# State-space convolution gated with linear attention, one core: inputs turned by TensorE instead of by DMA, the query side in blocks of 512 rows beside the first kernel channels, ScalarE table groups given explicitly

## The chip, the cores and the metric

One NeuronCore of one Trainium2 chip runs the whole program. The metric is the device time of one execution in microseconds (us). A profiled execution comes with it: its span goes from the first to the last instruction, and its whole time is a little longer. The engines are PE (TensorE; PEld is its weight loading), DVE (VectorE), ACT (ScalarE), POOL (GpSimd) and SP (SyncE); each has its own queue and works it off in order. "ACTq" and "SPq" are the queues' DMA issues.

## The reference

Two sequence operators on the same x (2048 rows, 512 columns, bf16), mixed by a gate per row:

```python
x = A_u
g = sigmoid((x * gate_w).sum(-1, keepdims=True))
# A: long convolution, its kernel K from a diagonal state space (128 states a channel)
dt = exp(log_dt)[:, None]; logdA = dt * (A_re + 1j * A_im); dB = dt * (B_re + 1j * B_im)
K = einsum("dn,dnl,dn->dl", C_re + 1j * C_im, exp(logdA[:, :, None] * arange(L)), dB).real
a = irfft(rfft(pad(x.T)) * rfft(pad(K)))[:L].T + x * Dskip
# B: linear attention, 32 heads of 16, features softmax(+p) and softmax(-p)
q, k, v = split(x @ wqkv); pq = q @ w_phi; pk = k @ w_phi
phi = lambda p: concat([softmax(p), softmax(-p)])
kv = einsum("sf,sd->fd", phi(pk), v); z = phi(pk).sum(0)
b = ((phi(pq) @ kv) / (phi(pq) @ z + 1e-6)) @ wo
return g * a + (1 - g) * b
```

## The kernel before

**Convolution.** It is a Fourier transform made of matmuls: stage a (`fft_stage_a`) multiplies with W1, stage b (`fft_stage_b`) with the tables TB, and each result is cast from PSUM to SBUF by an `Evict`, which gives its casts to DVE ("v", L68) and ACT ("a", L70) by a pattern. The input's spectrum XU is made once (`u_path`: 16 tiles of stage a into XAu, 16 of stage b into XU), from UD, which holds x with 64 rows per partition. The convolution kernel K is made for 128 channels at a time (`Q`, four blocks). For a block: E, the exponentials (L277, eight ACT tiles), and cs, the sines (L286 and L287, eight ACT tiles), from `args` on PE; then in four chunks of 32 channels R from E and cs (L296 to L300, DVE) and A from the tables C and D (L310 to L312, DVE, two buffers); kps from A and R on PE (L324), cast to KD; stage a into XA. Then four spectrum steps (`k_spectrum_inverse`): psB on PE, XK by ACT, two products t on DVE (L386, L387), psz on PE (L395), Z by ACT. Z goes out to Zd in DRAM and comes back turned as ZT (L402, L407, SP's queue). `k_out` starts psy with the attention's rows bS (L417), adds ZT times TJ (L420), DVE scales by the gate into ot (L423), and SP stores it (L426). XU waits in SBUF for all four blocks.

**Parameters.** C and D come from `compute_polar`, in two halves of 256 channels: products, logarithms and exponentials, one Arctan, four trig steps (fill, round, subtract on DVE; Abs and two Sin on ACT; L242 to L247), and products. Each half changes between ACT's table sets several times.

**Attention.** `attention` folds w_phi into the projections (Wkp, Wqp), makes the gates, and then takes the key side in eight turns of 256 rows (`s2`): pk on PE, Ek by ACT (L513), its sums Zk on DVE (L514), their reciprocal as Exp of minus Ln (L517, L518), v scaled to vr by DVE (L526), kvp on PE (L531). Each turn also does two parts of the query projection (pq, Eq; L498, L501). When kvp is complete, the scale factors of all queries are made at once (Zps, Sps, lnZ, den, apm; L558 to L577), Mw folds kv and wo, and for each of 4 blocks of 512 rows eight Eq tiles are scaled (aexp L595, L598) before four row groups of 128 are multiplied out (bps, L602 and L604) and stored to bSd (L696, L697).

**What sets the order.** The Python order gives priorities; the framework's scheduler places each instruction by them and by the tiles that are free, and writes one order per engine. A pool with one buffer a tag (ps0 in the first part: tag "pb") makes producer and consumer take turns. x comes in three times: as UD by POOL's DMA, copied to xp_d in another row order by ACT's DMA queue (L639), and from there turned into xT by SP (L654, DMA transposes); six parameter tensors and two weight blocks are DMA transposes too (L643, L652). An `ACT_TABLE_LOAD` is put in by the compiler before an activation whose function is not in the loaded set; `preload_act_table_set` names a set by hand.

Of the kernel before, what the change touches and what calls it, by code (L numbers as in the profile page):

```python
# [10 lines left out]
ACT = mybir.ActivationFunctionType  # L11
# [26 lines left out]
def build_index_cols(nc, pool):  # L38
# [15 lines left out]
    mk("h16", 4, 7); mk("s5", 5, 3); mk("b5", 5, 1)  # L54
# [18 lines left out]
def build_fft_consts(nc, persist, tp, ps_pool, icol, ident):  # L73
# [32 lines left out]
    for h in range(4):  # L106
        ps = ps_pool.tile([128, 4, 2, 64], F32, name="tips", tag="bk", bufs=2)
# [20 lines left out]
def build_selectors(nc, persist, tp):  # L128

    selE = persist.tile([128, 32, 64], BF16, name="selE")  # L130
    v64 = tp.tile([32, 32, 64], BF16, name="v64")
    iota_f(nc, v64[:], [[0, 32], [1, 64]])
    nc.gpsimd.tensor_scalar(out=v64[:], in0=v64[:], scalar1=1.0, scalar2=-31.5, op0=ALU.mult, op1=ALU.add)
    for sl in range(2):
        nc.gpsimd.affine_select(out=selE[32 * sl:32 * sl + 32, :, :], in_=v64[:], pattern=[[1, 32], [0, 64]],
                                compare_op=ALU.is_equal, fill=0.0, base=0, channel_multiplier=-1)
        nc.gpsimd.affine_select(out=selE[64 + 32 * sl:96 + 32 * sl, :, 0:32], in_=v64[:, :, 32:64], pattern=[[1, 32], [0, 32]],
                                compare_op=ALU.is_equal, fill=0.0, base=0, channel_multiplier=-1)
    return selE


def compute_params(nc, persist, tp, raw, A_re, A_im, log_dt, dram):


    kp = Bag()
    kp.stat = persist.tile([128, 16, 128], BF16, name="stat")
    kp.C = persist.tile([128, 2, 4, 512], BF16, name="Ctab")
    kp.D = persist.tile([128, 2, 8, 512], BF16, name="Dtab")


    ldc_b = tp.tile([128, 4], BF16, name="ldc_b")
    with nc.allow_non_contiguous_dma(reason="tiny"):
        nc.sync.dma_start(out=ldc_b[:], in_=log_dt.rearrange("(g p) -> p g", p=128))
    dtc = tp.tile([128, 4], F32, name="dtc")
    nc.scalar.activation(out=dtc[:], in_=ldc_b[:], func=ACT.Exp)
    pz = dram.tile([4, 512, 128], BF16, name="pz")
    for qi, (src, mul) in enumerate(((A_re, 1.0), (A_im, 1.0 / TWO_PI))):
        a = tp.tile([128, 4, 128], BF16, name=f"Ad{qi}")
        nc.sync.dma_start(out=a[:], in_=src.rearrange("(g p) n -> p g n", p=128))
        v = tp.tile([128, 4, 128], F32, name="p_v", tag="p_v")  # L160
        for g in range(4):
            nc.vector.tensor_scalar(out=v[:, g, :], in0=a[:, g, :], scalar1=dtc[:, g:g + 1], scalar2=mul, op0=ALU.mult, op1=ALU.mult)
        hl = tp.tile([128, 2, 4, 128], BF16, name="p_hl", tag="p_hl", bufs=2)
# [4 lines left out]
    for s in range(4):  # L168
        nc.sync.dma_start(out=kp.stat[32 * s:32 * s + 32, :, :], in_=pz[s].rearrange("(G p) n -> p G n", p=32))


    return kp


def compute_polar(nc, tp, kp, raw):
    for h in range(2):
        polar_half(nc, kp, tp, {k: v[:, 256 * h:256 * h + 256] for k, v in raw.items()}, slice(256 * h, 256 * h + 256))
    return kp


def polar_half(nc, kp, tp, raw, ds):
    nc.scalar.preload_act_table_set(LN_EXP)
    W = 256
    ld_b = raw["ld"]

    def T(name, dt=F32):
        return tp.tile([128, W], dt, name=name, tag="p512", bufs=9)
    Are, Aim, Bre, Bim, Cre, Cim = (raw[k] for k in ("Are", "Aim", "Bre", "Bim", "Cre", "Cim"))
# [23 lines left out]
    nc.scalar.activation(out=r[:], in_=r[:], func=ACT.Ln)  # L212
    nc.scalar.activation(out=r[:], in_=r[:], func=ACT.Exp, scale=-1.0)
# [571 lines left out]
```

## Time and profile before

| | us |
|---|---|
| median of 3 runs (lowest, highest) | 539.76 (539.34, 541.45) |
| the profiled execution | 540.47 |
| its span | 538.7 |
| PE busy / PEld busy | 297.7 / 166.6 |
| DVE busy / ACT busy / POOL busy | 283.1 / 278.2 / 21.5 |

A line of the timeline reads: start, length, engine, line of the code, operation, output<-input, shapes, count; in brackets, how long the engine had been idle and what ended that. Lines that follow each other on an engine overlap a little at their ends. A line of the stretches gives the busy time of every engine between two times. "L68" and "L70" are the two casts of `Evict` wherever they are used. Matmul ends are modelled, and a few per cent of the matmul records can be missing.

### The profile page before, as it was taken

Reading aid. Unit: us, or ns where it says so; the run is one execution under the profiler, and the core shown is the slowest. Engines: PE = TensorE matmul, PEld = TensorE weight load, DVE = VectorE, ACT = ScalarE, POOL = GpSimd, SP = SyncE. Lnnn points to the kernel's source line nnn. Section 1 sums busy time; section 2 is a strip of 40 time slices with the busy share of each in tenths; the row PEclk is TensorE's granted clock in tenths of the full one; section 3 lists DMA queues with packets and bytes.
Section 4 is the critical chain, followed back from the end, with each engine's and each line's share of the span. In section 5 each row is a group of like instructions: output and inputs, shape, how many; then the busy total and the mean of one; then the engine's idle time right before and its main releaser. Section 6 shows DMA issues by size and latency. Waiting matters only on the chain.

```text
span 538.7 us, 9011 instructions
## 1 busy us (share of the span) xinstructions
PE 297.7 (55%) x3845; PEld 166.6 (31%) x3856; DVE 283.1 (53%) x489; ACT 278.2 (52%) x359; POOL 21.5 (4%) x28
## 2 busy tenths in 40 slices
PE   0005442213787787499987447745785468646403
PEld 0004231101544343134332235224533353335201
DVE  2018755767656656433447972397319921951302
ACT  0025159895588988811229435943396239734000
POOL 6004300100000000000000000000000000000000
PEclk9999999999999999778985555555555555555555
DMA  9996300000000000001111004400185000580394
GB/s 153 153 286 122 78 1 2 0 0 1 1 1 1 0 2 0 1 24 45 49 41 40 1 2 79 80 1 12 21 168 40 1 6 13 153 67 2 78 144 54
DMA packets 64905, 25.90 MB, mean 48 GB/s; under 512 B 58177, under 2 KB 63297, under 8 KB 64865
## 3 DMA queue, kind: packets, MB, share of 16 engines
q1 hardware_dynamic: 62128, 21.00, 22.6%
q0 software_dynamic: 624, 2.23, 2.6%
q10 hardware_dynamic: 2112, 2.10, 1.2%
q8 instruction: 30, 0.49, 0.4%
q14 instruction: 11, 0.08, 0.1%
HBM read 12.47 MB, written 11.01 MB: 44 GB/s over the span
## 4 chain that ended last, share of the span: by engine, by line
ACT 30%; DVE 30%; PE 25%; SPq 8%; issue 4%; DMA 3%; ACTq 0%; DVEq 0%
PE psz L395 6%; PE bps L602 6%; ACT E L277 5%; SPq L643 3%; DVE A L312 3%; DVE A L310 3%; DVE Atmp L311 3%; ACT XK L70 2%; PE pk L511 2%; SPq L652 2%; DVE t L386 2%; PE psB L359 2%; PE psA L338 2%; DVE R L299 2%; ACT Z L70 2%
## 5 line engine op out<-in xcount | busy, mean ns | idle before, releaser
L395 PE MATMUL psz<-t,TI 64*128 64x128 bf16 x512 | 35.4, 305 | 30.7 <-DVE t L386 30.5
L338 PE MATMUL psA<-W,UD 128*64 128x256 bf16 x128 | 18.4, 422 | 56.6 <-DVE W L100 39.9
L359 PEld LDWEIGHTS <-TB 64*64 64x64 bf16 x960 | 26.0, 154 | 61.5 <-issue 61.5
L70 ACT CAST Z<-psz 128x1024 bf16<-128x1024 f32 x16 | 16.2, 1012 | 47.6 <-PE psz L395 47.6
L359 PE MATMUL psB<-XAu,TB 64*64 64x256 bf16 (+1 forms) x192 | 17.1, 484 | 42.8 <-DVE XU L68 19.2
L395 PEld LDWEIGHTS <-TI 64*128 64x128 bf16 x512 | 26.6, 133 | 35.3 <-issue 24.6
L386 DVE TENSOR_TENSOR t<-XU,XK 128x1024 bf16<-128x1024 bf16 x16 | 11.1, 691 | 47.1 <-ACT XK L70 47.1
L602 PE MATMUL bps<-Mw,Eq 128*128 128x512 bf16 x124 | 34.9, 429 | 0.9 <-DVE Eq L598 0.7
L423 DVE TENSOR_TENSOR ot<-psy,gT 128x512 bf16<-128x512 f32 x16 | 11.0, 690 | 44.5 <-PE psy L420 40.9
L598 DVE TENSOR_TENSOR Eq<-Eq,aexp 128x512 bf16<-128x512 bf16 x32 | 19.5, 679 | 26.7 <-PE aexp L595 26.7
L324 PE MATMUL kps<-R,A 128*32 128x64 bf16 x1024 | 21.2, 246 | 21.5 <-DVE A L312 18.5
L338 PEld LDWEIGHTS <-UD 128*64 128x64 bf16 x128 | 13.2, 205 | 60.3 <-issue 60.0
L277 ACT ACTIVATE E<-args 128x1024 bf16<-128x1024 f32 x32 | 30.1, 1052 | 2.9 <-PE args L275 2.9
L696 ACT CAST bs<-bps 128x512 bf16<-128x512 f32 x16 | 9.4, 586 | 42.3 <-PE bps L604 40.2
L526 DVE TENSOR_TENSOR vr<-vp,vr 128x512 bf16<-128x512 f32 x32 | 19.9, 682 | 16.6 <-ACT vr L518 16.6
L275 PE MATMUL args<-selE,stat 64*128 64x512 bf16 x64 | 27.2, 587 | 1.6 <-ACT E L277 0.9
L324 PEld LDWEIGHTS <-A 128*32 128x32 bf16 x1024 | 17.7, 151 | 31.6 <-DVE A L312 22.2
L335 PE MATMUL psA<-W,KD 128*128 128x256 bf16 x64 | 16.5, 413 | 19.8 <-ACT KD L70 19.8
L310 DVE TENSOR_TENSOR A<-Ctab,Dtab 128x1024 bf16<-128x1024 bf16 x32 | 21.5, 681 | 7.9 <-PE bps L604 7.9
L70 ACT CAST XA<-psA 128x1024 bf16<-128x1024 f32 x16 | 16.2, 1012 | 18.0 <-PE psA L335 18.0
L297 DVE TENSOR_TENSOR R<-E,cs 128x1024 bf16<-128x1024 bf16 x16 | 10.9, 684 | 26.1 <-ACT cs L286 26.0
L514 DVE TENSOR_REDUCE Zk<-Ek 128x64 f32<-128x1024 bf16 x16 | 19.3, 1218 | 8.5 <-ACT Ek L513 7.8
(200 smaller groups left out, 669.2 us busy)
## 6 DMA issues: line engine op xcount, KB each, us to landing
Zd<-Z SPq DMA_DIRECT2D x8, 512.0 KB, 4.8
ZT<-Zd SPq DMA_DIRECT2D x32, 128.0 KB, 5.1
xp_d<-in_A_u_dram ACTq DMA_DIRECT2D x4, 512.0 KB, 5.5
UD<-in_A_u_dram POOLq DMA_DIRECT2D x4, 512.0 KB, 17.1
bSd<-bs SPq DMA_DIRECT2D x16, 128.0 KB, 1.7
bS<-bSd SPq DMA_DIRECT2D x4, 512.0 KB, 4.5
out_dram<-ot SPq DMA_DIRECT2D x64, 32.0 KB, 1.6
Wv<-in_B_wqkv_dram SPq DMA_DIRECT2D x1, 512.0 KB, 4.5
```

Of the source, the lines that this page charges most:

```text
L70: self.nc.scalar.copy(out=out, in_=in_)
L275: nc.tensor.matmul(ps[:, 8 * j:8 * j + 8, :], lhsT=kp.stat[0:64, G0 + gi, :], rhs=selE[0:64, d0:d0 + 8, :], start=True, stop=True, tile_po ...
L277: nc.scalar.activation(out=E[:, 32 * gi + 16 * b2:32 * gi + 16 * b2 + 16, :], in_=ps[:], func=ACT.Exp)
L310: nc.vector.tensor_tensor(out=A[:, o], in0=Cb(i0), in1=Db(j0), op=ALU.mult)
L324: nc.tensor.matmul(kps[32 * dj:32 * dj + 32, g4, e, :], lhsT=A[:, ri, :, :, d].rearrange("p a b -> p (a b)"), rhs=R[:, ri, d, :], start=(r ...
L338: nc.tensor.matmul(ps[64 * e:64 * e + 64, i, :], lhsT=l[e], rhs=rhs, start=True, stop=True, tile_position=(0, 64 * e))
L359: nc.tensor.matmul(o, lhsT=fc.TB[rows, r, op, :], rhs=rhs, start=(op == 0), stop=(op == 2), tile_position=(64 * e, 64 * rpar), skip_group_ ...
L386: nc.vector.tensor_tensor(out=t12[:], in0=Us, in1=XK[:], op=ALU.mult)
L395: nc.tensor.matmul(psz[:, rpar, sl, :], lhsT=fc.TI[rows, rh0 + sl, b0:b0 + 2, :].rearrange("p a b -> p (a b)"), rhs=rhs, start=(op == 0), ...
L526: nc.vector.tensor_tensor(out=vr[:, u, sg, :, 0:128].rearrange("p m (h e) -> p m h e", e=16), in0=vp[:].rearrange("p (m h e) -> p m h e", ...
L598: nc.vector.tensor_tensor(out=e, in0=e, in1=ps[:], op=ALU.mult)
L602: nc.tensor.matmul(ps[:], lhsT=Eq[:, i // 4, i % 4, 128 * j:128 * j + 128], rhs=Mw[:, i, :], start=(i == 0), stop=False, skip_group_check= ...
```

## The change

It is a rewrite of the program's frame around the same arithmetic. Line numbers here are those of the new file where order rows are shown.

- Inputs: all loads stand on SP's queue and none is a transpose. The six parameter tensors come in as they lie and are turned by matmuls with the identity (L199); x is turned the same way from UD (`turn_x`, 64 matmuls and 8 casts into xT); the two weight blocks by `fold_projection`. xp_d is gone. w_phi comes in one DMA.
- Parameters: one pass over 512 channels; the trig steps still go in halves. The selector selE is made by DVE instead of POOL.
- Table groups: `Tables` names the set by hand (`begin`) and binds each Exp, Ln, Sin and Arctan behind its group's load. ACT's order has 11 table loads, 45 before.
- PSUM: psP (two buffers, tag "pb") for the whole program, psA (three) for the attention, psF (two, tag "fb") for the spectra and the output once psA is closed. `u_path` works in two halves of the channels.
- Key side: kvp in 32-row pieces (64 small matmuls a turn where 16 larger ones were), no query work inside.
- Query side: `query_block` does 512 rows from pq to the stores; two blocks, then the first channel block's E and cs, then the other two blocks and the first channel block's `kgen` together.
- Channel loop: spectrum and output of block Q come first, then the tables and `kgen` of Q + 1; R and XA have two buffers from then on; KD takes two chunks at once; output in 8 row groups at a time, not 4.

The core of the diff:

```diff
+class Tables:
+    def begin(self, name):
+        p = self.nc.scalar.preload_act_table_set(name)
+        order_after(self.tc, p, self.cur)
+        self.head, self.cur = p, [p]
...
+    def __call__(self, **kw):
+        i = self.nc.scalar.activation(**kw)
+        order_after(self.tc, i, self.head)
...
+def turn_x(nc, UD, xT, ident, psP, ev):
+    for T in range(8):
+        ps = psP.tile([128, 8, 4, 32], F32, name="xps", tag="pb")
+        for t in range(8):
+            nc.tensor.matmul(ps[:, t, :, :], lhsT=UD[:, 8 * T + t, :], rhs=ident[:], start=True, stop=True)
+        ev(xT[:, :, 256 * T:256 * T + 256].rearrange("p k (t q) -> p t k q", q=32), ps[:])
...
+def query_block(nc, act, at, qp, psA, xT, Wqp, Mw, b, sink):
+    Eq = []
+    for mp in range(2):
+        e = qp.tile([128, 2, 2, 512], BF16, name="Eq", bufs=3)
...
+    act(out=lnZ[:], in_=zs[:, 0:2, :], func=ACT.Ln)
+    act(out=den[:], in_=lnZ[:], func=ACT.Exp, scale=-1.0)
...
+    act(out=apm[:], in_=lnZ[:], func=ACT.Exp, scale=-1.0)
+    for i in range(4):
+        j = 4 * b + i
+        for mp in range(2):
+            ps = psA.tile([128, 2, 2, 128], F32, name="aexp", tag="bk")
...
+            nc.vector.tensor_tensor(out=e, in0=e, in1=ps[:], op=ALU.mult)
+        ps = psA.tile([128, 512], F32, name="bps", tag="bk")
...
-        for J in range(4):
-            nc.scalar.dma_start(out=xp_d[512 * J:512 * J + 512, :].rearrange("(jc q) d -> jc q d", q=32), in_=xv[16 * J:16 * J + 16])
...
-            nc.sync.dma_start_transpose(out=raw[k][:].unsqueeze(1), in_=src)
+            nc.sync.dma_start(out=rawd[k][:], in_=src.rearrange("(g p) n -> p g n", p=128))
...
+        for b in range(2):
+            query_block(nc, act, at, qp, psA, xT, Wqp, Mw, b, sink)
+        tabs = kgen_tables(0)
+        act.begin(LN_EXP)
+        for b in range(2, 4):
+            query_block(nc, act, at, qp, psA, xT, Wqp, Mw, b, sink)
+        XA = kgen(0, tabs)
+        ca.close()
...
         for Q in range(4):
...
+            k_spectrum_inverse(nc, fc, XA, nd, tpool, XU, d0, Z, Zd, ZT, psF, "fb", eva, eva, 2)
+            k_out(nc, fc, ident, ZT, nd, d0, bS, gT, out2d, opool, psF, "fb")
+            if Q < 3:
+                tabs = kgen_tables(Q + 1)
+                act.begin(LN_EXP)
+                XA = kgen(Q + 1, tabs)
```

ACT in the middle of the key side, before; one turn:

```order
L513 ACTIVATE Ek<-pk 128x512 x4
L517 ACT_TABLE_LOAD
L517 ACTIVATE Zk<-Zk 128x128
L518 ACT_TABLE_LOAD
L518 ACTIVATE vr<-Zk 128x16x8
L501 ACTIVATE Eq<-pq 128x512 x4
```

The same engine now, the last turn of the key side and what follows it (E and args belong to the first channel block):

```order
L96 ACTIVATE Ek<-pk 128x512 x4
L96 ACTIVATE Zk<-Zk 128x128
L96 ACTIVATE vr<-Zk 128x64x2
L96 ACTIVATE E<-args 128x1024 x3
L611 CAST KVT<-ktp 128x512 x2
L616 CAST Mw<-mps 128x512 x8
L96 ACTIVATE E<-args 128x1024
L96 ACTIVATE Eq<-pq 128x512 x8
```

Both loads and the four Eq of a turn are gone from it; Eq comes eight at a time in the query blocks, behind Mw.

ACT in the channel loop before, from the end of one spectrum into the next block's tables:

```order
L70 CAST XK<-psB 128x1024
L277 ACT_TABLE_LOAD
L277 ACTIVATE E<-args 128x1024
L70 CAST Z<-psz 128x2x4x128
L277 ACTIVATE E<-args 128x1024 x7
L286 ACT_TABLE_LOAD
```

ACT in the channel loop now, from the end of block 1's kernel (KD, XA) over block 2's tables into block 1's spectrum (XK, Z):

```order
L70 CAST KD<-kps 128x1024
L70 CAST XA<-psA 128x64x16 x2
L96 ACTIVATE E<-args 128x1024 x8
L91 ACT_TABLE_LOAD
L96 ACTIVATE cs<-args 128x1024 x8
L91 ACT_TABLE_LOAD
L70 CAST XK<-psB 128x1024
L70 CAST KD<-kps 128x1024
L70 CAST Z<-psz 128x2x4x128
```

The tables of block 2 stand ahead of the spectrum of block 1, and that spectrum lies among block 2's kernel; in the loop before, a block's spectrum stood ahead of the next block's tables.

DVE at the end of the program, before (t of the last block, then its outputs):

```order
L387 TENSOR_TENSOR t_5382<-XU,XK 128x1024
L386 TENSOR_TENSOR t_5470<-XU,XK 128x1024
L387 TENSOR_TENSOR t_5471<-XU,XK 128x1024
L423 TENSOR_TENSOR ot<-psy,gT 128x512 x8
L780 UNCONDITIONAL_BRANCH
```

DVE there now, from the last spectrum step of block 2 (t_5424) into the first steps of block 3 (t_6014 on):

```order
L423 TENSOR_TENSOR t_5424<-XU,XK 128x1024
L424 TENSOR_TENSOR t_5425<-XU,XK 128x1024
L462 TENSOR_TENSOR ot<-psy,gT 128x1024
L423 TENSOR_TENSOR t_6014<-XU,XK 128x1024
L424 TENSOR_TENSOR t_6015<-XU,XK 128x1024
L423 TENSOR_TENSOR t_6103<-XU,XK 128x1024
L424 TENSOR_TENSOR t_6104<-XU,XK 128x1024
L462 TENSOR_TENSOR ot<-psy,gT 128x1024
```

An output of block 2 now stands ahead of block 3's first products; PE's order has the psy of block 2 directly ahead of the psB of block 3 in the same way.

More of the change, by code (lines that the diff above doesn't have):

```diff
@@ L106, in build_fft_consts @@
     for h in range(4):
[L107 removed]
+        ps = ps_pool.tile([128, 4, 2, 64], F32, name="tips", tag="pb")
         for r4 in range(4):
@@ L142, in compute_params @@
[L142 to L153, printed above, removed]
+    c32 = tp.tile([128, 32], F32, name="c32")
@@ L168, in compute_params @@
     for s in range(4):
[L169 to L188, printed above, removed]
+        nc.sync.dma_start(out=stat[32 * s:32 * s + 32, :, :], in_=pz[s].rearrange("(G p) n -> p G n", p=32))
```

729 lines of the change are left out of this document (395 added, 334 removed).

## The prediction

> **What bounds the kernel now.** I read the page first, then busy time by stretch, the timeline around each boundary, and the chain of waits.
>
> ```profile
> span 538.7 us, 9011 instructions
> ACT 30%; DVE 30%; PE 25%; SPq 8%; issue 4%; DMA 3%; ACTq 0%; DVEq 0%
> ```
>
> ```profile
> 0.00:54.30 54.30, 8.51 (x104) 6.62 (x105) 18.23 (x39) 10.74 (x11) 15.00 (x21) 1.00 0.97 177
> 147.00:211.00 64.00, 51.45 (x323) 25.93 (x322) 38.07 (x49) 56.92 (x94) 0.00 (x0) 1.00 0.00 1
> 229.00:281.00 52.00, 48.39 (x220) 20.78 (x224) 20.08 (x33) 9.70 (x17) 0.00 (x0) 0.86 0.12 38
> 338.00:395.00 57.00, 36.14 (x684) 21.66 (x683) 33.71 (x56) 31.46 (x35) 0.00 (x0) 0.50 0.16 30
> ```
>
> The columns of the second fence are start:end, length, busy time of PE, PEld, DVE, ACT and POOL, granted clock, DMA share, GB/s. No engine bounds the whole: the chain passes from ACT to DVE to PE. In the key side (147 to 211) ACT is busy 56.92 of 64 us; in the query side (229 to 281) PE is, 48.39 of 52; in a channel block (338 to 395) nobody, 36 of 57 at best. So each stage is priced by itself. I cut the run into five: **A** start to the last cast of XU, **B** folds, gates and key side, **C** query side and first channel kernels, **D** from the first psB to the last Z, **E** the tail.
>
> The start, in the timeline:
>
> ```profile
> 0.80 33.97 ACTq L639 DMA_DIRECT2D xp_d<-in_A_u_dram  x4
> 34.80 1.28 ACT L182 ACT_TABLE_LOAD   x1 [34.80 <-DMA gw<-in_gate_w_dram]
> ```
>
> Four DMA issues hold ACT's queue 34 us, and ACT's first instruction starts at 34.80. Next the u path, the trig steps of the parameters, and the end of A:
>
> ```profile
> 61.57 1.12 PE L338 MATMUL psA<-W,UD 128*64 128x256 bf16 x8 [2.62 <-DVE XAu L68]
> 62.73 1.01 ACT L70 CAST XAu<-psA 128x1024 bf16<-128x1024 f32 x1 [4.95 <-PE psA L338]
> 64.95 1.23 DVE L68 CAST XAu<-psA 128x1024 bf16<-128x1024 f32 x1 [1.47 <-PE psA L338]
> ...
> 119.98 0.43 DVE L233 SCALAR_TENSOR_TENSOR u<-neg,cbi 128x256 f32<-128x256 f32 x1 [1.30 <-ACT cbi L231]
> 130.89 0.89 DVE L259 TENSOR_SCALAR big_a<-are 128x256 f32<-128x256 f32 x4
> 135.77 1.04 ACT L247 ACTIVATE trg<-big_n 128x1024 bf16<-128x1024 f32 x1
> ...
> 141.27 1.01 ACT L70 CAST XU<-psB 128x1024 bf16<-128x1024 f32 x1 [3.56 <-PE psB L359]
> ```
>
> Matmuls (1.12) and casts (1.01 or 1.23) take turns: one PSUM tile. One trig step runs from 130.89 to 136.81, 5.9 us. A ends at 142.3. One turn of the key side, eight in all:
>
> ```profile
> 160.60 0.31 ACT L517 ACTIVATE Zk<-Zk 128x128 f32<-128x128 f32 x1
> 162.43 2.04 ACT L501 ACTIVATE Eq<-pq 128x512 bf16<-128x512 f32 x4
> 162.56 2.48 DVE L526 TENSOR_TENSOR vr<-vp,vr 128x512 bf16<-128x512 f32 x4 [2.02 <-ACT vr L518]
> 165.97 2.56 DVE L514 TENSOR_REDUCE Zk<-Ek 128x64 f32<-128x1024 bf16 x2 [0.92 <-ACT Ek L513]
> 167.29 1.28 ACT L517 ACT_TABLE_LOAD   x1
> 168.58 0.31 ACT L517 ACTIVATE Zk<-Zk 128x128 f32<-128x128 f32 x1
> ```
>
> A turn lasts 8.0 us (from Ln at 160.60 to Ln at 168.58); two loads take 2.57 of it and the four Eq exponentials 2.04, and DVE needs 5.04 (vr 2.48, Zk 2.56). The last vr, six turns after the one at 162.56, ends B at 213.2. Then the query side:
>
> ```profile
> 227.82 1.06 ACT L577 ACTIVATE apm<-lnZ 128x1024 bf16<-128x1024 f32 x1
> 232.67 4.57 PE L602 MATMUL bps<-Mw,Eq 128*128 128x512 bf16 x11
> 251.97 0.59 ACT L696 CAST bs<-bps 128x512 bf16<-128x512 f32 x1 [0.73 <-PE bps L604]
> 253.67 1.89 PE L602 MATMUL bps<-Mw,Eq 128*128 128x512 bf16 x8
> 253.92 0.59 ACT L696 CAST bs<-bps 128x512 bf16<-128x512 f32 x1 [1.36 <-PE bps L604]
> L324 PE MATMUL kps<-R,A 128*32 128x64 bf16 x1024 | 21.2, 246 | 21.5 <-DVE A L312 18.5 <-DVE R L300 2.9
> 314.43 1.07 PE L359 MATMUL psB<-XA,TB 64*64 64x128 bf16 x48 [1.10 <-ACT XA L70]
> ```
>
> In a block a row group takes 1.95 us (251.97 to 253.92). After the pause that ends with apm, 11 matmuls took 4.57 us, 0.415 each, against 0.236 later (1.89 for 8): a restart costs about 2 us. C ends at 314.4 with the first psB. The channel loop:
>
> ```profile
> 336.81 6.53 ACT L277 ACTIVATE E<-args 128x1024 bf16<-128x1024 f32 x7
> 345.71 0.69 DVE L297 TENSOR_TENSOR R<-E,cs 128x1024 bf16<-128x1024 bf16 x1 [12.02 <-ACT cs L286]
> 359.10 0.68 DVE L300 TENSOR_TENSOR R<-E,ns 128x1024 bf16<-128x1024 bf16 x1
> 359.70 0.68 DVE L310 TENSOR_TENSOR A<-Ctab,Dtab 128x1024 bf16<-128x1024 bf16 x1
> 489.66 1.68 PE L395 MATMUL psz<-t,TI 64*128 64x128 bf16 x28
> 486.27 1.01 ACT L70 CAST Z<-psz 128x1024 bf16<-128x1024 f32 x1 [3.18 <-PE psz L395]
> 491.38 1.01 ACT L70 CAST Z<-psz 128x1024 bf16<-128x1024 f32 x1 [3.18 <-PE psz L395]
> 501.51 1.01 ACT L70 CAST Z<-psz 128x1024 bf16<-128x1024 f32 x1 [3.09 <-PE psz L395]
> ```
>
> E is exponentiated at 0.93 us a tile, then a load, then cs; DVE had waited 12.02 us for it. DVE's products follow each other at 0.60 us. A spectrum step is 5.1 us (486.27 to 491.38), four to a block. The last Z ends D at 502.5. And the tail:
>
> ```profile
> 514.67 0.43 SPq L402 DMA_DIRECT2D Zd<-Z  x1
> 521.77 1.89 SPq L407 DMA_DIRECT2D ZT<-Zd  x4
> 526.25 0.62 PE L420 MATMUL psy<-ZT,TJ 64*32 64x128 bf16 x16 [9.47 <-DMA ZT<-Zd]
> out_dram<-ot SPq DMA_DIRECT2D x64, 32.0 KB, 1.6
> ```
>
> The last line is the page's: issues, size, us to landing. From the issue of Zd to psy's first matmul on the reloaded ZT are 11.6 us; E lasts 36.2 us (502.5 to 538.7).
>
> **The change part by part.**
>
> A, 142 us, to about 117. With no DMA on ACT's queue its first Sin can start as soon as DVE has made tg_v. DVE's constants are its busy time to 54.3 less two casts of XAu at 1.23, 15.8, plus the selector that POOL made before (two products' worth, 1.2), plus some 5 of waits for the Sin tiles: they end at about 23. Rates, products, logarithms and the two exponential groups are a chain of some 30 instructions of 512 columns; 256 take 0.43 and a cast of 1024 takes 1.23, so 0.77 with the hand-off: to 46. Four trig steps at 5.9, with eight xT casts (1.01 or 1.23), four casts of the first fold and some 18 products of 0.6 sharing the two engines, take 33: to 79. The u path comes behind all this in the new order of ACT and DVE (before it lay beside the parameters), 32 casts in two PSUM tiles. A pair costs at least 1.23 + 0.6 + 0.1 = 1.95 if PE runs twice as fast as at 61.57, at most 1.23 + 1.12 + 0.1 = 2.45: 31 to 39 us; I take 37, nearer the row. The input transposes on PE (turn_x, 64 matmuls of 128 columns, and the folds' 32) are bounded by nothing and by 96 x 0.14 = 13 us (1.12 for eight of 256 columns); PE has nothing else to do beside the trig steps, so I take nothing, and 6 if that cover is gone. DMA: 5 MB at the 177 GB/s of the first stretch would be 28 us and the weights are needed at about 70, so none on the path. A: -25.
>
> B, 71 us, to 50. No loads and no Eq remain in a turn. ACT needs 2.0 + 0.6, DVE 5.04 plus the wait for Ln and Exp between Zk and vr (2 x 0.31 and hand-offs, 0.9), since Zk and vr alternate in DVE's order. So a turn is 5.9; PE's 16 matmuls of 512 columns (0.236 each, 3.8) and 64 small ones for kvp (not in the trace; kps, 21.2 us for 1024, is the nearest: 1.3) fit in it. 8 x 5.9 = 47, less 1 for work done ahead, plus 4 for the query fold. B: -21. Removed here are 16 loads of 1.28 by the row: 20.5. The Trainium skill ("ScalarE: Activation LUTs", "What ACT_TABLE_LOAD costs") has about 2.66 us for a switch, load and drain; by it these 16 would be worth 42.6 and the whole would end 22 us earlier. In the trace the instruction after a load starts 0.02 behind it (167.29 + 1.28, then 168.58), so the drain is not seen and the row decides.
>
> C, 101 us, to 120: dearer. fold_kv first: four small products at 0.4, ten casts of 0.59 into KVT and Mw: 8. Then per block, one after another, because PE's order has pq of block b+1 behind bps of block b: pq and eight Eq at 0.51 with zs, 5.9; the chain lnZ, den, products, apm, seven steps of 256 columns at 0.43 + 0.1, 3.7, in which PE stands; restart 1.7 to 2; four row groups. A row group was 1.95 with all of Eq scaled ahead. Now aexp of group j+1 is queued behind bps of j, so PE waits for one product: 0.25 + 0.2 + 0.7 + 0.1 + 2.1 = 3.35. Block: 5.9 + 3.7 + 13.4 + 1.8 = 24.8. Block 0 carries five E tiles in its chain (+3), block 1 eight cs tiles and two loads between the bs casts (+2); blocks 2 and 3 the tables: DVE has batches of four or five products (2.4 to 3 us) ahead of each pair of Eq products, where some 2 us are free, so +0.85 a group, +1.5 in the chain: 29.6 each. 8 + 28 + 26.8 + 29.6 + 29.6 = 122, less 2 as fold and E overlap: 120. What is bought: the first channel block's tables, 33 us before (281 to 314.4), lie inside. C: +19.
>
> D, 188 us, to 185. Spectrum 0 now runs with the next tables: 24 ACT tiles at 0.95, two loads, waits: 27. Kernel 1: four chunks of ten products and one ns, 25.4, started 7 before the spectrum's end, plus 3.6 to the last XA: 22. Then E of block 2 stands in ACT's queue behind the last XA of block 1: 10.6 (8 x 0.93, 1.28, two cs) in which DVE can do two chunks of A, no more (two buffers); then R 11, two chunks of A 7.2, eight t 4.8, two ot 2.4, drain 2.7: 39 with kernel 2 and spectrum 1. The same for block 3 without a spectrum but with nearly all of A: 10.6 + 11 + 13.2 + 2.7 + 1 = 38.5. Spectra 2 and 3 come last, with nothing beside them: 4 x 5.1 + 3 and 4 x 5.1 + 2. Between them PE's queue has psy of block 2, which waits for ZT: Z to Zd to ZT, 11.6 + 0.9. Queued behind it on PE are the psB of spectrum 3, and ACT and DVE wait for those. 27 + 22 + 39 + 38.5 + 23.5 + 12.5 + 22.5 = 185. D: -3.
>
> E, 36 us, to 20.5: bS loads early and the last Zd no longer stands behind sixteen output DMAs on SP's queue (Z ended at 502.5, Zd was issued at 514.67). 12 for Zd and ZT, two psy and ot 3.6 (1.23 for an ot), eight issues of 0.43, 1.6 to land. E: -16.
>
> Sum: 538.7 - 25 - 21 + 19 - 3 - 16 = 492.7. The profiled execution took 540.47, 1.8 over its span and 0.7 over the median of the runs, 539.76; so 492.7 + 1.8 - 0.7 = 493.8, forecast **494**. What each term may miss (u path 6, rest of A 8, B 5, C 15, D 10, E 4), squared and added, gives 21 either way: 473 to 515.
>
> **The rivals.**
>
> *Half clock through the attention (slower).* If the four pauses of about 4 us pull PE's clock down and the stretches between are too broken to bring it back, 512 columns cost 0.415: B's turn becomes PE's, 16 x 0.415 + 1.7 = 8.4, +20; a block gains 10 x 0.18 x 4 for bps and aexp, 3 for pq, 1 for zs, +11, four times 44. 558. It decides against the change from about 46 of those 64 us on, that is, with the clock at 0.50 in more than two thirds of it. For it: the loop's 0.50 with PE busy 36 of 57 us, never recovering. Against: 1.00 at 51 of 64, and 0.86 overall right after a pause. 6%, and 4% for a part of it that just cancels the gain. The Trainium skill ("TensorE: Matmul & The Clock Gate", "HAM oscillation") says that one idle window of 3.4 us halves the clock and one busy window restores it; by it the blocks would start slow and recover each time, the 2 us that the sum has, and this rival would not occur. The loop's row does not bear out the second half: hence 10%, not less.
>
> *Tables not hidden.* If the 44 products of the first channel block delay the Eq products one for one, C is 44 x 0.6 - 10 = 16 longer: 510. DVE's order puts them directly ahead; the free time per group is my estimate. 20%.
>
> *PE faster.* If denser work brings the clock up in the u path and in spectra 2 and 3 (psz 1.68 to 0.9, psB 1.07 to 0.5 in each of eight steps, and 6 in the u path), 494 - 6 - 11 = 477, and less ACT queueing of E than its order suggests would give 465. 15%.
>
> *The change does not do what it says.* If the loads came back between Zk and vr, B would keep 20 us: 514. The order shows none there. 2%.
>
> **How the numbers follow.** Forecast 53%, tables not hidden 20, PE faster 15, half clock 10, loads back 2. Faster by over 0.5% (about what a measurement of this kernel can tell from no change) are all but the half clock's cases: 0.90; same 0.04; slower 0.06. The range reaches from 468, inside the fast case, to 525, beyond the two middling ones.
>
> **What would show it.** ACT's first load at about 1 us and the last XU near 117; turns of 5.9 in the key side with no load in it; row groups of 3.4 and a pause of some 4 us before each block's aexp, with the clock low only there; DVE waiting for cs about 10 us twice; a PE wait of about 12 for ZT ahead of the last spectrum. Wrong it is if C takes over 140, if the clock stays at 0.50 in B, or if spectra 2 and 3 overlap anything.

## The result

Before: 540.2 us, median of 4 runs (539.3 to 541.5). After: **475.5 us**, median of 4 (475.3 to 478.2), ratio 0.881 with an interval of 0.878 to 0.885. The forecast was 494, 468 to 525: faster, inside the range, and 18 us too long. The profiled execution took 475.32 us, 1.8 over its span.

The page's head and chain after the change:

```profile
span 473.5 us, 10567 instructions
DVE 36%; PE 33%; ACT 24%; DMA 3%; issue 3%; SPq 0%; POOL 0%; ACTq 0%; DVEq 0%; POOLq 0%
```

DVE now leads the chain, then PE; ACT, level with DVE before, is third. By stage, cut as in the prediction (each end is the start of a row below plus its length):

| stage | before | forecast | after |
|---|---|---|---|
| A, to the last cast of XU | 142.3 | 117 | 109.1 |
| B, to the last vr | 70.9 | 50 | 51.1 |
| C, to the first psB | 101.2 | 120 | 108.6 |
| D, to the last Z | 188.1 | 185 | 188.2 |
| E, tail | 36.2 | 20.5 | 16.6 |

(ACT's order has 12 table loads after the change, not the 11 told above.)

The timeline of the changed kernel, in the columns of before (start, length, engine, line, operation, idle before it): the start, the end of A, two key turns, the query blocks, the last XA of block 2 and the tail.

```profile
3.82 0.55 ACT L96 ACTIVATE w<-tg_v,mpi 128x32 bf16<-128x32 int32 x2 [1.80 <-DVE m L125]
...
71.23 0.68 DVE L290 TENSOR_TENSOR Dtab<-Dtab,trg 128x1024 bf16<-128x1024 bf16 x1
...
74.62 1.02 ACT L70 CAST XAu<-psA 128x1024 bf16<-128x1024 f32 x1 [1.03 <-issue]
...
87.82 0.64 PE L390 MATMUL psB<-XAu,TB 64*64 64x256 bf16 x24 [0.46 <-ACT XU L70]
...
107.83 1.23 DVE L68 CAST XU<-psB 128x1024 bf16<-128x1024 f32 x1 [0.74 <-PE psB L390]
...
151.86 2.49 DVE L580 TENSOR_TENSOR vr<-vp,vr 128x512 bf16<-128x512 f32 x4 [0.72 <-ACT vr L96]
155.71 1.22 DVE L568 TENSOR_REDUCE Zk<-Ek 128x64 f32<-128x1024 bf16 x1 [0.23 <-ACT Ek L96]
157.65 2.48 DVE L580 TENSOR_TENSOR vr<-vp,vr 128x512 bf16<-128x512 f32 x4 [0.72 <-ACT vr L96]
...
169.07 2.75 PE L629 MATMUL pq<-xT,Wqp 128*128 128x512 bf16 x12
181.68 3.60 PE L668 MATMUL bps<-Mw,Eq 128*128 128x512 bf16 x8 [0.36 <-DVE Eq L664]
186.85 1.90 PE L668 MATMUL bps<-Mw,Eq 128*128 128x512 bf16 x8 [0.56 <-DVE Eq L664]
195.26 3.62 PE L629 MATMUL pq<-xT,Wqp 128*128 128x512 bf16 x16
204.08 1.00 PE L661 MATMUL aexp<-apm,Xsel 32*128 32x256 bf16 x4 [3.27 <-ACT apm L96]
205.44 3.59 PE L668 MATMUL bps<-Mw,Eq 128*128 128x512 bf16 x8 [0.36 <-DVE Eq L664]
219.28 3.62 PE L629 MATMUL pq<-xT,Wqp 128*128 128x512 bf16 x16
243.71 3.62 PE L629 MATMUL pq<-xT,Wqp 128*128 128x512 bf16 x16
268.69 0.67 PE L390 MATMUL psB<-XA,TB 64*64 64x128 bf16 x48
...
359.22 1.93 ACT L70 CAST XA<-psA 128x1024 bf16<-128x1024 f32 x2
...
422.91 0.34 SPq L439 DMA_DIRECT2D Zd<-Z  x1
430.95 1.04 PE L459 MATMUL psy<-ZT,TJ 64*32 64x128 bf16 x32 [7.01 <-DMA ZT<-Zd]
...
455.87 1.01 ACT L70 CAST Z<-psz 128x1024 bf16<-128x1024 f32 x1 [3.79 <-PE psz L432]
456.91 0.34 SPq L439 DMA_DIRECT2D Zd<-Z  x1
463.70 1.04 PE L459 MATMUL psy<-ZT,TJ 64*32 64x128 bf16 x32 [5.75 <-DMA ZT<-Zd]
```

ACT's first Sin is at 3.8; before, its first instruction of all was at 34.80. In the u path 24 matmuls take 0.64 us, and DVE's casts follow every 1.96 us, 1.23 and 0.74 of waiting. A key turn lasts 5.79 (151.86 to 157.65, one vr batch to the next) with no load and DVE idle 0.95 of it. In a query block the first row group's eight bps take 3.6 us (181.68, 205.44), later ones 1.90. In block 1 they come behind a pause in which PE idles 3.27 us (204.08). In block 0 matmuls of `args` lie in that place, no wait of PE there is longer than 0.62 us, and the first group is just as slow. Blocks start at 169.07, 195.26, 219.28 and 243.71. Busy time by stretch (columns as before):

```profile
195.00:219.00 24.00, 19.77 (x173) 9.47 (x172) 12.38 (x22) 18.11 (x26) 0.00 (x0) 0.86 0.07 23
312.54:323.40 10.86, 8.74 (x19) 2.06 (x18) 0.01 (x1) 10.11 (x11) 0.00 (x0) 0.50 0.01 2
311.00:330.00 19.00, 14.06 (x119) 4.63 (x121) 6.78 (x13) 18.23 (x20) 0.00 (x0) 0.50 0.00 1
432.00:457.00 25.00, 14.48 (x355) 11.81 (x356) 7.53 (x10) 8.01 (x8) 0.00 (x0) 0.50 0.30 65
```

Up to 269 us the granted clock is 0.94 on average, and 0.86 in the query stretch shown; in the three later stretches it is 0.50, as in the channel loop before. From 311 to 330 ACT is busy 18.2 of 19 us, nearly all with tables, and DVE waits 12.2 of them for the first cs. DVE's waits for cs in the whole run (engine, waited for, us in total, times, longest):

```profile
DVE R L342 <- ACT cs L96: 29.1, 4, 14.5
```

### The profile page after: what moved, and what is told of

It reads as the page before. It is cut to its first block, busy times and chain, and to the rows that moved or that the text cites. A ratio compares the mean times of both kernels' runs of the same rounds, so it can differ in the third digit from the quotient of the medians.

```text
span 473.5 us, 10567 instructions
## 1 busy us (share of the span) xinstructions
PE 291.6 (62%) x4712; PEld 173.2 (37%) x4712; DVE 284.5 (60%) x479; ACT 241.6 (51%) x318; POOL 7.2 (2%) x19
## 4 chain that ended last, share of the span: by engine, by line
DVE 36%; PE 33%; ACT 24%; DMA 3%; issue 3%; SPq 0%; POOL 0%; ACTq 0%; DVEq 0%; POOLq 0%
PE bps L668 8%; PE psz L432 4%; ACT E L96 4%; ACT Eq L96 3%; ACT Z L70 3%; ACT XK L70 3%; PE psB L390 3%; PE pk L565 2%; DVE A L331 2%; PE args L301 2%; DVE Atmp L330 2%; DVE Zk L568 2%; DVE A L329 2%; DMA ZT<-Zd 2%; DVE vr L580 2%
## 5 line engine op out<-in xcount | busy, mean ns | idle before, releaser
L432 PE MATMUL psz<-t,TI 64*128 64x128 bf16 x512 | 31.1, 292 | 24.2 <-DVE t L423 23.1
L356 PE MATMUL kps<-R,A 128*32 128x64 bf16 x1024 | 22.5, 241 | 26.6 <-DVE R L345 17.5
L668 PE MATMUL bps<-Mw,Eq 128*128 128x512 bf16 x128 | 37.1, 443 | 2.5 <-DVE Eq L664 2.4
L513 PE MATMUL xps<-ident,UD 128*128 128x128 bf16 x64 | 7.8, 307 | 40.6 <-ACT xT L70 29.3
L356 PEld LDWEIGHTS <-A 128*32 128x32 bf16 x1024 | 20.0, 151 | 33.7 <-issue 22.1
L96 ACT ACTIVATE cs<-args 128x1024 bf16<-128x1024 f32 x32 | 30.4, 1053 | 0.5 <-PE args L311 0.5
L664 DVE TENSOR_TENSOR Eq<-Eq,aexp 128x512 bf16<-128x512 bf16 x32 | 20.6, 685 | 16.7 <-PE aexp L661 16.6
L462 DVE TENSOR_TENSOR ot<-psy,gT 128x1024 bf16<-128x1024 f32 x8 | 9.8, 1224 | 30.0 <-PE psy L459 30.0
L70 ACT CAST XK<-psB 128x1024 bf16<-128x1024 f32 x16 | 16.3, 1020 | 18.1 <-PE psB L390 18.0
L96 ACT ACTIVATE Ek<-pk 128x512 bf16<-128x512 f32 x32 | 17.3, 594 | 13.1 <-PE pk L565 13.1
L330 DVE TENSOR_TENSOR Atmp<-Ctab,Dtab 128x1024 bf16<-128x1024 bf16 x32 | 22.1, 692 | 0.3
L331 DVE TENSOR_TENSOR A<-A,Atmp 128x1024 bf16<-128x1024 bf16 x32 | 22.1, 692 | 0.3
```

The source lines that it names most:

```text
L70: self.nc.scalar.copy(out=out, in_=in_)
L96: i = self.nc.scalar.activation(**kw)
L330: nc.vector.tensor_tensor(out=tmp[:], in0=Cb(i1), in1=Db(j1), op=ALU.mult)
L331: nc.vector.tensor_tensor(out=A[:, o], in0=A[:, o], in1=tmp[:], op=op)
L356: nc.tensor.matmul(kps[32 * dj:32 * dj + 32, g4, e, :], lhsT=A[:, ri, :, :, d].rearrange("p a b -> p (a b)"), rhs=R[:, ri, d, :], start=(r ...
L432: nc.tensor.matmul(psz[:, rpar, sl, :], lhsT=fc.TI[rows, rh0 + sl, b0:b0 + 2, :].rearrange("p a b -> p (a b)"), rhs=rhs, start=(op == 0), ...
```

## Experiments

All but the last ran once: one profile and one time. Four runs of the changed kernel spread over 3 us, so smaller differences of the whole time are not read. Differences are to the changed kernel's 475.5 us unless another number is named. The kernel before, run beside them, took 540.4 us with e1 to e4, 542.2 with e5 to e8 and 543.3 with e9 to e11, so that against 475.5 the results of e7 to e11 may be up to 3 us too long.

**e1: table loads back into the key side.**

```diff
+        act.begin(LN_EXP)
         act(out=Zk[:], in_=Zk[:], func=ACT.Ln)
+        act.begin(LN_EXP)
         act(out=vr[..., 32:34], in_=Zk[:]..., func=ACT.Exp, scale=-1.0)
```

> The changed kernel with two table loads put back into each of the eight key turns, one ahead of Ln and one ahead of the Exp behind it; nothing else. Theory (the loads lie on the chain Zk - Ln - Exp - vr that DVE waits for): a turn goes from 5.8 to 5.8 + 2 x 1.28 = 8.4 us, eight turns +20.5, the time 475.5 + 20.5 = 496. Rival (ACT has room, 22.9 of 51 us busy in this stage, and DVE or PE sets the turn): turns stay near 5.8 and the time stays within 3 us of 475.5; then the gain of this stage came from the Eq exponentials that left it.

485.7 us, +10.2: half of the theory's 20.5, and more than the rival's 3. One turn, on ACT and on DVE:

```profile
135.04 1.28 ACT L91 ACT_TABLE_LOAD   x1
136.67 1.28 ACT L91 ACT_TABLE_LOAD   x1
137.96 0.32 ACT L96 ACTIVATE vr<-Zk 128x128 bf16<-128x128 f32 x1
142.08 1.28 ACT L91 ACT_TABLE_LOAD   x1
135.06 1.22 DVE L568 TENSOR_REDUCE Zk<-Ek 128x64 f32<-128x1024 bf16 x1 [0.18 <-ACT Ek L96]
```

The load at 135.04 runs while DVE still sums the second Zk (135.06 to 136.28), so Ln starts when it would have without it. Only the load at 136.67 lengthens the way to vr: a turn is 7.04 (135.04 to 142.08), 1.25 more.

**e2: the copy of x back on ACT's queue.**

```diff
+        for J in range(4):
+            nc.scalar.dma_start(out=xp_d[512 * J:512 * J + 512, :]..., in_=xv[16 * J:16 * J + 16])
         act.begin(TRIG)
```

> The changed kernel with the four DMA issues that copy x to scratch DRAM put back at the head of ACT's queue; nobody reads the copy. Theory (ACT's free queue is what the front end gained): ACT's first Sin moves from 3.8 us to about 36, the constants, the parameter chain and the u path follow it, less some 6 us in which casts of xT fill waits; the last XU near 109 + 26 = 135 and the time near 501. Rival (the start is bound by DVE, 48.5 of the first 60 us busy, or by the u path's PE work): last XU below 119, time below 485.

488.6 us, +13.1: neither.

```profile
0.72 9.33 ACTq L732 DMA_DIRECT2D xp_d<-in_A_u_dram  x4
28.85 0.69 DVE L477 TENSOR_TENSOR Wphi<-wc,mask 128x512 bf16<-128x512 bf16 x1 [11.15 <-DMA wc<-in_B_w_phi_dram]
```

The four issues held ACT 9.3 us, not 34. The first Sin is 7.6 later; the rest is another thing: with ACT late, the planned order put Wphi early on DVE (28.85 us, 55.43 without the copy), where it waited 11.15 us for wc, whose DMA was itself issued 6.4 us later on SP's queue. So this run does not price the queue.

**e3: the first channel kernel behind the query blocks.**

```diff
-        tabs = kgen_tables(0)
-        act.begin(LN_EXP)
         for b in range(2, 4):
             query_block(nc, act, at, qp, psA, xT, Wqp, Mw, b, sink)
+        tabs = kgen_tables(0)
+        act.begin(LN_EXP)
```

> The changed kernel with the tables' Sin group and all products of the first channel block put behind the fourth query block instead of beside blocks 2 and 3. Theory (the products lie free beside the row groups, whose 3.2 us are PE's bps and one Eq product): the blocks keep their 24.0 to 24.4 us, the products left behind (some 34 at 0.6, plus waits) come on top, first psB near 268.7 + 21 = 290, time near 497. Rival (the forecast's prices: 0.85 us a row group and 1.5 us of chain in each of the two blocks beside the tables): those blocks fall to about 19.5, and the time is near 487.

500.7 us, +25.3, and the theory's 497 is the nearer. Block 2, now without products:

```profile
222.71 3.62 PE L629 MATMUL pq<-xT,Wqp 128*128 128x512 bf16 x16
246.41 3.62 PE L629 MATMUL pq<-xT,Wqp 128*128 128x512 bf16 x16
```

Block 2 lasts 23.7 (222.71 to 246.41), against 24.4 with the products beside it (219.28 to 243.71). Hiding the tables costs block 2 0.7 us, not the 4.9 that the forecast charged. Block 1, without its cs tiles and the first products, lasts 23.5 for 24.0: 0.5 us, not the 2 of the forecast. What hiding saves is some 20 us of stage C: that stage is 21.5 longer here, of which 1.7 come from a second slow row group in block 0, which the edit does not touch.

**e4: the u path on one PSUM tile.**

```diff
...
-        u_path(nc, fc, UD, xau, XU, psP, ev, 2)
+        cq.close()
+        cq = ExitStack()
+        u_path(nc, fc, UD, xau, XU, pool(cq, "psU", 1, space=PSUM), ev, 2)
...
```

> The changed kernel with the u path on one PSUM tile instead of two; the folds and transposes keep two. Theory (two tiles let ACT's and DVE's casts run side by side, 0.98 us a cast; the matmuls stay at 0.64 to 0.9 for 24 or 8): with one tile a cast costs 0.7 + 1.12 + 0.2 = 2.0, 32 casts +33 us, the time 508. Rival A (the double rate of PE in this stage came from the density of its work, and goes with it): matmuls back to 1.12, 2.45 a cast, +46, time 521. Rival B (the stage is bound by the parameters ahead of it): less than +10.

517.4 us, +42: nearest rival A as a number.

```profile
95.77 1.07 PE L390 MATMUL psB<-XAu,TB 64*64 64x256 bf16 x24 [1.33 <-DVE XU L68]
100.34 1.07 PE L390 MATMUL psB<-XAu,TB 64*64 64x256 bf16 x24 [1.32 <-DVE XU L68]
```

and, by stretch:

```profile
91.00:109.00 18.00, 8.55 (x192) 7.11 (x192) 4.61 (x5) 4.05 (x4) 0.00 (x0) 0.50 0.01 2
```

A pair of casts takes 4.57 here (95.77 to 100.34) instead of 1.96. The u path lasts 71.6 us from its first cast for 34.4, +37; another 4 of the 42 lie in stage B, whose second fold and first key turn begin with PE at half rate. The 24 matmuls take 1.07; with two tiles they take 0.64, and here the granted clock is 0.50. The rate falls on the way: the first four sets of psA matmuls take 0.72, from 81.87 us on they take 1.12, though PE never idles longer than 1.4 us. The first pair, still at the full rate, takes 3.85. So some 1.8 of the 2.6 us a pair are the waits of a single tile (the theory), and 0.8 is the slower PE that follows from them (rival A).

**e5: the kernel before without the copy of x.** Leaves out the reordering, so the columns of xT stand in another order.

```diff
-        for J in range(4):
-            nc.scalar.dma_start(out=xp_d[512 * J:512 * J + 512, :]..., in_=xv[16 * J:16 * J + 16])
-            nc.sync.dma_start_transpose(..., in_=xp_d[512 * J:512 * J + 512, :])
+            nc.sync.dma_start_transpose(..., in_=x2d[512 * J:512 * J + 512, :])
```

> The kernel before without the four DMA issues on ACT's queue: the copy of x in another row order is left out, and the transposing loads of xT read x itself, so that xT's columns stand in another order. Theory (ACT's held queue is what the old start lost): ACT's first Sin goes from 37.4 to about 10 us, where DVE has tg_v, and stage A and the whole get 20 to 27 us shorter: 513 to 520. Rival (after e2, where the same four issues held ACT only 9.3 us: the start is bound by the transposing loads on SP's queue and by what is issued behind them, Ad at 49.1): ACT starts early but waits for the loads; the whole gains less than 12: over 528.

527.6 us beside 542.2: -14.6, between the two.

```profile
43.06 0.20 ACT L155 ACTIVATE dtc<-ldc_b 128x4 f32<-128x4 bf16 x1 [9.55 <-DMA ldc_b<-in_A_log_dt_dram]
126.50 1.01 ACT L70 CAST XU<-psB 128x1024 bf16<-128x1024 f32 x1 [3.56 <-PE psB L359]
```

The first Sin starts at 11.0, but dtc waits at 43.06 for a load issued on SP's queue behind the transposing loads. The last XU ends at 127.5 for 142.3. So in that kernel the copy and the queue it held cost 15 of the 33 us by which stage A shrank. The loads behind the transposes and the u path's single tile are candidates for the rest; no run takes them out of the kernel before.

**e6: the kernel before with one table group in the attention.**

```diff
...
-    nc.scalar.preload_act_table_set(LN_EXP)
...
+    act = Tables(tc, LN_EXP, LAST)   # ahead of the gates, behind the last Sin; all activations go through act
```

> The kernel before with one explicit table group (Ln and Exp) on ACT from the gates to the end of the attention, which removes 20 loads there and nothing else; the four Eq exponentials stay in each key turn. Theory (from e1: a load ahead of Ln is covered by DVE's second Zk, one ahead of Exp is not; but here ACT is busy 56.9 of 64 us, so both count): turns of 8.0 fall to DVE's 5.9 or a little above, 6.2, eight turns -14, four loads in the softmax chain -5: 521. Rival (half is covered, as in e1): turns of 6.8, -10 - 5, 525, and the Eq exponentials are the other half of what stage B gained. Second rival (PE or PSUM tiles set the turn): over 533.

524.6 us beside 542.2: -17.7, the number and the turn of the first rival.

```profile
156.56 2.56 DVE L534 TENSOR_REDUCE Zk<-Ek 128x64 f32<-128x1024 bf16 x2 [0.67 <-ACT Ek L196]
163.24 2.56 DVE L534 TENSOR_REDUCE Zk<-Ek 128x64 f32<-128x1024 bf16 x2 [0.92 <-ACT Ek L196]
```

and that turn as a stretch:

```profile
156.56:163.24 6.68, 6.62 (x42) 3.38 (x41) 4.92 (x6) 4.74 (x10) 0.00 (x0) 1.00 0.00 1
```

Turns are 6.68 (156.56 to 163.24): without the loads a turn is 1.3 of the 2.2 us shorter. What ends the gain there is PE, busy 6.62 of the 6.68 us, as the second rival has it, while ACT is busy 4.74. DVE waits 0.7 to 0.9 for Ek, and ACT in turn waits for PE's pk. So the other 0.9 came when the query work left the turn, its matmuls on PE (pq, 1.89 a turn) first of all; what its Eq exponentials on ACT cost by themselves is not shown.

**e7: outputs later.** psy of a block moves into the next block's spectrum.

```diff
             rs = slice(r0, r0 + step)
+            if r0 == 0 and late:
+                late()               # bS load and k_out of the block before
...
+            late = lambda d0=d0: outs(d0)
...
```

> The changed kernel with the output matmuls (psy) and the load of bS of each channel block written two spectrum steps later, inside the next block's spectrum, just ahead of its first ZT; one ZT and one bS tile for all. Theory (psy waits for ZT, and stands ahead of the next spectrum's psB in the PSUM ring and in PE's order; that holds spectra back until no tables are left to run beside them): the wait of 8 us ahead of the last spectrum goes, and spectra 1 and 2 move beside the next tables, where DVE waited 29 us for cs: -8 -12, about 455. Rival (stage D is the chain of tables, ACT's E and cs behind the last XA, and the spectra would not fit beside them): only the 8 us go, 467, or less.

464.4 us, -11: between the two, nearer the rival. Stage D fell by 16 (first psB 267.6, last Z 439.9), but the tail grew to 22.5:

```profile
427.30 12.83 SPq L467 DMA_DIRECT2D out_dram<-ot  x8
447.60 1.89 PE L457 MATMUL psy<-bS,ident 128*128 128x512 bf16 x4 [8.72 <-DMA bS<-bSd]
```

Eight output DMAs now stand on SP's queue ahead of the last block's first Zd. The second four of them wait for their ot (ready at 438.3), so that both halves of Zd go out together at 440.2, and bS, queued behind them, comes 8.7 us late.

**e8: PE kept busy in the query pauses.**

```diff
             ps = psA.tile([128, 2, 2, 128], F32, name="aexp", tag="bk")
+            for f in range(14 if i + mp == 0 else 0):
+                nc.tensor.matmul(ps[:]..., lhsT=Wqp[:, f % 4, 0:128], rhs=xT[:, f % 4, 0:512], start=True, stop=True)
```

> The changed kernel with 14 matmuls of 512 columns added in each query block into the first aexp tile, ahead of its real matmuls, so that PE works through the pause in which zs, lnZ, den and apm are made; their results are overwritten. Theory (the pause drops the clock, and the first row group of a block pays for it: its eight bps take 3.6 us, the next ones 1.9): the first group falls to 1.9, 4 x 1.7 = 6.8 less, 468.5. Rival (the added 14 x 0.24 = 3.4 us are longer than the free time, or run at half rate, 5.9, and delay aexp): no gain or up to 8 us slower, 476 to 484.

471.9 us, -3.6, of which stage C has 4.7 (103.9 for 108.6): some two thirds of the theory.

```profile
203.58 1.90 PE L670 MATMUL bps<-Mw,Eq 128*128 128x512 bf16 x8 [0.56 <-DVE Eq L666]
215.62 3.62 PE L629 MATMUL pq<-xT,Wqp 128*128 128x512 bf16 x16
238.37 3.62 PE L629 MATMUL pq<-xT,Wqp 128*128 128x512 bf16 x16
264.89 0.67 PE L390 MATMUL psB<-XA,TB 64*64 64x128 bf16 x48 [0.33 <-ACT XA L70]
```

The first eight bps take 1.90 in all four blocks now (203.58 is block 1), and block 2 lasts 22.8 for 24.4. So the missing work on PE ahead of it is the cause of the slow first group, at some 1.7 us a block. The last block lost it again (238.4 to 264.9, 26.5 us, for 25.0): there the channel kernel's products end last.

**e9: e7 with two bS tiles and outputs on POOL's queue.**

```diff
-                nc.sync.dma_start(out=ov[c, :, j0:j0 + nj, :], in_=ot...)
+                nc.gpsimd.dma_start(out=ov[c, :, j0:j0 + nj, :], in_=ot...)
...
+            bS = fpool.tile([128, 16, nd], BF16, name="bS", bufs=2)
```

> e7 with two bS tiles, each loaded at the start of its block again, and the output DMAs issued from POOL's queue instead of SP's. Theory (in e7 eight output DMAs held SP's queue 12.8 us ahead of the last Zd, and bS came 8.7 us late, so that the tail grew from 16.6 to 22.5): the tail falls to 16, ZT of block 2 is back sooner, the time 464.4 - 6 - 4 = 454. Rival (the tail is the way of Z to Zd to ZT itself, and POOL's issues are no faster than SP's): 460 to 465.

457.0 us: between the two, nearer the theory. Stage D is down to 163.5 (272.4 to 435.8), the tail to 18.7, not to 16.

**e10: PE kept busy in the last two spectra.**

```diff
+        for f in range(5 if d0 >= 2 * nd else 0):
+            nc.tensor.matmul(psz[:, 0, :, :], lhsT=fc.TI[:, f, 0:2, :]..., rhs=XU[:, f, 0, :], start=True, stop=True)
```

> The changed kernel with five matmuls of 512 columns added ahead of the real ones in each psz tile of the last two spectra, overwritten by them. Theory (in these steps PE waits so much that it runs at half rate: psB 1.07 us, psz 2.1; kept busy it runs at full rate): psB 0.6 and psz 1.2, eight steps of -1.4, 464.5; this is what the forecast's rival 'PE faster' had counted on for these spectra. Rival (the stage stays at half rate, and five cold matmuls of 0.42 fill the 1.9 us that PE waits there and a little more): 475 to 478.

468.8 us, -6.7: between the two. Stage D has 4.3 of it (267.7 to 451.6); the rest lies in A and E, outside the two spectra of the edit.

```profile
400.42 2.29 PE L427 MATMUL psz<-XU,TI 128*128 128x512 bf16 x5 [1.11 <-ACT XK L70]
410.23 1.24 PE L427 MATMUL psz<-XU,TI 128*128 128x512 bf16 x5 [0.26 <-ACT Z L70]
```

The rate rises (five added matmuls 2.29, then 1.24), but each spectrum's first step or two are still slow (2.29 again at 431.37) and pay for the added work. The half rate there is real and can be mended; it is worth 4 us, not 11.

**e11: tables early.**

```diff
...
+                if early:            # in kgen, after each pair of chunks
+                    nxt[0].extend(kgen_exp(... 4 * Q + 4 + i) for i in (2 * c2, 2 * c2 + 1))
+                    if c2 == 1:
+                        act.begin(TRIG)
+                        nxt[1].extend(kgen_trig(... 4 * Q + 4 + i) for i in range(4))
...
```

> e9 with the tables of channel blocks 2 and 3 written into the kernel stage of the block before: two E after its second chunk, the other two and cs after its fourth, ahead of that block's spectrum. Theory (what is left of stage D is DVE's wait for cs at the head of each block, 12.3 us in e7, longest 8.6): the waits go, 8 to 12 us less than e9. Rival (E and cs now stand ahead of XK on ACT and hold the spectrum back, 10.6 us each time, with nothing else for DVE to do): as e9 or up to 10 us slower than it.

448.3 us, 8.8 less than e9, but not for the reason given:

```profile
DVE t L423 <- ACT XK L70: 34.2, 10, 6.1
DVE R L342 <- ACT cs L96: 17.9, 2, 9.2
```

The waits for cs grew from 8.6 to 17.9; those for XK fell from 45.5 to 34.2; the spectra now lie mostly beside the next products instead of beside tables, which is the likely reason. Of the 8.8, stage D has 4.3 (159.2 for 163.5). The other 4.4 lies ahead of the first psB, where the two kernels have the same code: 1.4 in A, 1.8 in B, and 1.3 in C, where e9 has a second slow row group. I read that as scatter, and the edit as worth about 4.

**e12: together, four runs.**

> e11 with the added matmuls of e8 (14 in each query block's pause) and of e10 (five ahead of each psz of the last two spectra). Theory (three separate causes: the order of outputs and tables, the restart after each query pause, the half rate in the last spectra): the gains add, 448.3 - 3.6 - 5 = 440, a little less than e10 alone as part of spectrum 2 now lies beside tables. Rival (with the order mended DVE and ACT set these stages, and the faster PE only waits): 445 to 449.

447.2 us (445.9 to 448.0), ratio to before 0.824 (0.821 to 0.826): the fastest here, and no faster than e11. The first psB came 3.7 earlier (264.3 for 268.0), and the time was lost again at once, by the table load that ends block 1's tables (290.8 for 291.2). The stretch between the two:

```profile
264.30:290.80 26.50, 17.22 (x410) 11.31 (x410) 12.43 (x21) 23.69 (x26) 0.00 (x0) 0.78 0.45 105
```

ACT, with the tables of block 1 and the casts of spectrum 0, is busy 23.7 of these 26.5 us (in e11 22.6 of 23.2), PE 17.2: a PE that arrives sooner waits for ACT. The rival held.

## Why the prediction came out as it did

The whole came out 18 us below the forecast: A, C and E were 8, 11 and 4 us shorter than summed, B 1 and D 3 us longer.

- **A, -33 for -25.** The direction was right; the chain of parameters was mis-sized: the constants were done at 16.8 on DVE, forecast 23 (its terms add to 22), and the chain behind them ("four trig steps ... to 79") kept that lead: its last product ends at 71.9. The u path took 34.4 from its first cast (74.6), forecast 37; its pairs came at the lower bound, 1.95, since the matmuls of a tile took 0.64 to 0.72 for 1.07 to 1.12. The forecast took 37, near the upper bound, as "nearer the row", but that row belonged to a PE that waited between single tiles (e4). How the 18 us beyond e5's 15 split between parameters and u path is open: before, the two lay beside each other.
- **The rival "PE faster"** named 477, and the time was 475.5, but that is luck. It held in the u path alone, for 2.6 of its 6 us. Its other 11 were to come from spectra 2 and 3, and those stayed at half rate: psB takes 1.07 there at a granted clock of 0.50.
- **B, -20 for -21.** Right in sum; a turn is 5.79 for 5.9. The split was priced wrong: 16 loads counted in full are 20.5 us, but two loads back in a turn cost 1.25, not 2.57 (e1), because one of the two lies beside DVE's Zk. Loads back cost 10 us, not the 20 of that rival. In the kernel before, a turn without loads stops at PE's 6.62 us of work (e6), so the rest of the 2.2 us a turn came with the query work that left it. The row of a load held: in e1 the Exp starts 0.01 behind one (136.67 + 1.28, then 137.96). The 2.66 us of the Trainium skill ("ScalarE: Activation LUTs", "What ACT_TABLE_LOAD costs") is not borne out.
- **C, +7 for +19.** The failed step is "blocks 2 and 3 the tables: +0.85 a group, +1.5 in the chain". They took 24.4 and 25.0 for 29.6 each. A group leaves DVE 1.94 us idle (block 0, without tables), the planned order put three or four products there, and e3 measures 0.7 us for block 2. Blocks 0 and 1 were 1.8 and 2.8 us shorter than summed; the cs tiles charged to block 1 at 2 cost 0.5. The restart is confirmed (3.6 for 1.90, and e8), and half clock through the attention did not occur. The clock came back after each slow group, as the Trainium skill has it ("TensorE: Matmul & The Clock Gate", "What's actually happening"). Its other half, an idle window of about 3.4 us that halves the clock, is not borne out in block 0, where PE never waited longer than 0.62 us.
- **D, 0 for -3.** The sum came near because its terms missed in both directions. The step that failed is the overlap "10.6 ... in which DVE can do two chunks of A": while DVE waited for cs it did none of A's products (busy 0.01 of 10.86 us in the stretch from 312.54), since R, which needs cs, stood ahead of them in its order. From block 1's last XA (312.5) to block 2's (361.2) it took 48.6 us for the 39 of the sum. Against that, spectrum 0 and kernel 1 took 43.9 for 49, and the way from the last Z of block 2 to the next psB 10.4 for 12.5 (Zd issued at 422.91, psy at 430.95: 8.0 for 11.6). As forecast, spectra 2 and 3 ran at half rate with nothing beside them, and DVE waited twice for cs, 12.2 and 14.5 us for 10.6. What the forecast saw as a wait between two spectra is larger: psy's place ahead of the next psB holds spectra back while tables run (e7, e9: 16 and 25 us of stage D).
- **E, -20 for -16.** From Zd's issue to the first psy on the reloaded ZT 6.8 us (456.91 to 463.70), not 11.6, with nothing else on the queue.

## What to carry to other kernels

A table load, or any step, costs what sticks out behind the partner's work: read which of two loads the other engine was waiting for before multiplying by their number. Price PE's steps in a stage by how long PE will wait there, not by a row from a stage where it waited differently. Before work is counted as hidden behind a wait, see that it stands ahead of the waiting instruction in its engine's order. And where outputs of one block share PSUM tiles and a queue with the next block's first step, place them by what they wait for, not by where the loop ends.

## What the hardware showed

- A pause of 3.3 us nearly doubled the time of the next eight matmuls, 1.90 to 3.59 us (block 1). Thin work did the same without a pause: in block 0 PE was busy 2.8 of the 5 us from 175.3 to 180.3, and the next eight took 3.60. Added matmuls in that place kept them at 1.90 (e8). In block 0 of e3 and e9 the second group was slow too (3.48 and 3.41) behind the same work: the slow stretch has no fixed length.
- In the kernel before, busy time by stretch gives a granted clock of 1.00 for the stretch that holds the eight psA matmuls of 1.12 us:

```profile
60.00:84.00 24.00, 10.10 (x72) 7.29 (x72) 13.34 (x27) 11.49 (x19) 0.00 (x0) 1.00 0.19 44
```

  In e4 the same eight take 1.12 (from 109 us on) at a granted clock of 0.50. From 0 to 20 us of the kernel before, with no matmul at all, it reads 1.00 as well. Where PE is mostly idle that column is no witness for its rate.
